# Three edits to the order of work in the attention stage: VectorE's late work in slots 0, 5 and 9, the loads of the value weights, and one matmul of the last two units

## The chip, the cores and the metric

The kernel runs on one core of a Trainium2 chip. The metric is device time in microseconds (us) of one launch; a number of launches gives a median. A core has five engines that each work through their own list of instructions in order and wait for one another by semaphores: TensorE (PE, with PEld for its weight loads), VectorE (DVE), ScalarE (ACT), GpSimd (POOL) and SyncE (SP), which here only issues DMAs. Matmuls write to PSUM, eight banks of 128 x 512 fp32; DVE and ACT read it. Everything else lies in SBUF, and what does not fit goes through DRAM by DMA.

## What is computed

One transformer block in fp32: a layernorm, attention with 32 heads of width 20 over a sliding window of 256 positions, and a gated MLP on the normed input, both added to the input.

```python
def _A_ref(x, wqkv, wo):
    H = 32; Dh = D // H; W = 256
    qkv = (x @ wqkv).reshape(B, S, 3, H, Dh).transpose(2, 0, 3, 1, 4)
    q, k, v = qkv[0], qkv[1], qkv[2]
    scores = jnp.einsum("bhqd,bhkd->bhqk", q, k) * (Dh ** -0.5)
    idx = jnp.arange(S)
    mask = (idx[:, None] - idx[None, :] >= 0) & (idx[:, None] - idx[None, :] < W)
    scores = jnp.where(mask[None, None], scores, -1e9)
    p = _softmax(scores, axis=-1)
    o = jnp.einsum("bhqk,bhkd->bhqd", p, v)
    return o.transpose(0, 2, 1, 3).reshape(B, S, D) @ wo

xn = _layernorm(x, axis=-1)
return x + _A_ref(xn, wqkv, wo) + (_gelu(xn @ w_gate) * (xn @ w_up)) @ w_down
```

S is 2048, D is 640 and the MLP is 1728 wide.

## The kernel before

An fp32 product is made of three matmuls on operands that are split into a high and a low part (`dense_steps`, L104: high by high, low by high, high by low, five column blocks each, so 15 matmuls to a group). The program has three stages: layernorm with the first projections (to about 99 us of the span), attention (to about 534 us), and the rest of the MLP with the output projection. The change touches the attention stage alone.

**Units and slots.** `attention` (L836) walks through 32 units, eight groups of four heads by four chunks of 512 positions, and each unit has `NS` = 14 slots. Time in units is read from the products of probabilities with values (ps_o on PE, `av_unit`), which come once a unit in its slot 0: unit 8 begins at 199.3 us of the profile, unit 19 at 352.5, unit 20 at 366.8. In every slot the loop first runs what falls due (`tick`), then in slots 0, 5 and 9 two pairs of score blocks for the row maxima (`pull_max`, `max_pair`), in odd slots two pieces of exponentials (`exp_piece`: two matmuls to a PSUM tile ps_e, then ACT's exp into P), then `flush`, then some matmuls of a **filler** (`pull_fill`): the dense groups of the projections and of the MLP's first tiles, which do not depend on the attention. `RATE` over `NS` says how many filler matmuls a slot gets; `debt` carries the fraction. In slot 1 one more filler matmul is pulled (L874) and in slot 3 the debt is lowered by one (L879).

**The order is written out by hand.** On PE, ACT, DVE, POOL and SP the instructions run in the order in which the program issues them (`manual_schedule`, L894), so an instruction that waits holds up all that stand behind it on its engine.

**PSUM.** Four banks (`psm`) are taken in turn by the score blocks of the maxima, two to a pair, and by a small transpose ps_n in slot 7. A pair's banks are free when DVE's two reductions (L537, junk<-ps_m) have read them. Slot 0 has up to four pairs: two ahead of the ps_o products and two behind them, so the fourth pair takes the banks of the second. Two banks (`psx`) are shared by ps_e and ps_o, two (`psd`) by the dense groups.

**What follows a dense group.** For queries and keys (`save_qk`, L262): `upper` on ACT (L291, pt<-ps_d) one slot after the group, `middle` on DVE (L287, r<-ps_d,pt), `lower` on ACT (L269, pt<-r) some slots later by the table `LAG`, `lowest` on POOL (L273, pt<-r,pt), then the stores by SP. The tile r has one buffer: the next `middle` writes r when the `lowest` before it has read it. For the MLP (`gate_up_fill`, L679): `c1` on ACT, `c2` on DVE, `c3` on ACT, `c4` on DVE (L701, gs<-ps_d,gs), `c5` on DVE (L708, he<-he,gs), then a store. DVE's part of this is called **late** work: `late` (L212) puts it on the list `lates`, and `flush` (L218) issues the list at the end of the slot.

**Loads.** SP issues all DMAs of this stage but one. `load_stack` brings queries and keys (qs, ks) back from DRAM, three units ahead, keys in slot 9 and queries in slot 12. `av_unit` stores its result from ob in slot 6 (od, sd; ob is first joined by POOL, L645). The weights of the second half of the values come through `load_v` (L296), a generator that the filler advances: its first step loads two blocks of 160 KB into two buffers wvr, each further step converts one block on ACT (L315, wvh<-wvr) and POOL (L316) and loads another; the five blocks are converted in units 5 to 8, the last two of them both in unit 8.

Of the kernel before, what the change touches and what calls it, by code (L numbers as in the profile page):

```python
# [30 lines left out]
NS = 14  # L31
# [4 lines left out]
KSLOT = 9  # L36
LAG = 3, 5, 4, 4, 4, 4, 3, 3, 4, 3, 2, 1, 1, 1
NFA = 3
HD = D // 2
HR = 5  # L40
NQD = 9
# [26 lines left out]
def block_kernel(ctx, tc, x, wqk, wv, wgu, wdo, wdl, out):  # L68
    nc = tc.nc
# [21 lines left out]
    td = [{i: dram.tile([128, 2, C], F32, name=f"td{p}{i}") for i in (1, 2, 3, 4)} for p in range(NC // 2)]  # L91
    wtd = [dram.tile([128, 4, HD], F32, name=f"wtd{q}") if q not in OWN else None for q in range(NQD)]
    rd = [dram.tile([H, C], F32, name=f"rd{c}") for c in range(NC)]
# [111 lines left out]
    now = [None]  # L205

    def at(slot, fn, *a):
        acts.setdefault(slot, []).append((fn, a))

    lates = []  # L210
# [7 lines left out]
    def flush():  # L218
        while lates:
            fn, a = lates.pop(0)  # L220
            fn(*a)

    def lag():
        return 1 if now[0] is None or now[0] < NS else LAG[now[0] % NS]

# [70 lines left out]
    def load_v(h, res, rpool=None, vt=None):  # L296
        wh = wvp.tile([128, KT, 320], F32R, name="wvh", tag="wvh")
        wl = wvp.tile([128, KT, 320], F32R, name="wvl", tag="wvl")

        if rpool is not None:  # L300
            rall = rpool.tile([128, KT, 320], F32, name="wvall")
            nc.sync.dma_start(rall, wv[h])

        def get(k):
            if rpool is not None:
                return rall[:, k, :]
            raw = wvp.tile([128, 320], F32, name="wvr", tag="wvr", bufs=2)
            nc.sync.dma_start(raw, wv[h, :, k, :])
            return raw
        raws = [get(0), get(1)]  # L310
        yield
        for k in range(KT):
            if rpool is None and 0 < k < KT - 1:
                raws.append(get(k + 1))
            nc.scalar.activation(wh[:, k, :], raws[k], AF.Copy)  # L315
            nc.gpsimd.tensor_tensor(out=wl[:, k, :], in0=raws[k], in1=wh[:, k, :].bitcast(F32), op=OP.subtract)  # L316
            if rpool is not None and k + 2 < KT:
                raws.append(get(k + 2))
            yield
        res.append((wh, wl, vt or v_tiles()))  # L320

    def v_tiles():
        vt = []
        for g in range(4):
            v = vp.tile([128, VW], F32, name="v", tag="v")
            nc.gpsimd.memset(v[:, NB * 84:NB * 84 + 12], 0.0)
            nc.gpsimd.memset(v[:, 0:NB * 84].rearrange("p (b j d) -> p b j d", j=4, d=21)[:, :, :, 20:21], 1.0)
            vt.append(v)
        return vt
# [17 lines left out]
    def run(*gens):  # L347
        for gen in gens:
            for _ in gen:
                pass  # L350
# [142 lines left out]
    def load_stack(u, which=(0, 1)):  # L493
        g, c = divmod(u, NC)
        for m in range(80 * g // 128, (80 * g + 79) // 128 + 1):
            assert all((m + 5 * i, c) in done for i in which), (u, m)

        for i in which:
            dst, src, top, again = ((qs[u % NQ], qd[c], 1, 2), (ks[u % NK], kd[c], 0, 0))[i]
            for j in (0, 2):  # L500
                for p, part, n in ((j * 32, top, 2), (j * 32 + 2 * DH, again, 1), (64 - j * 32, 0, 3)):
                    nc.sync.dma_start(dst[p:p + DH * n, j:j + 2].rearrange("p j t -> p (j t)"),
                                      src[g, part:part + n].rearrange("s (d j) t -> (s d) (j t)",
                                                                      j=4)[:, j * C:(j + 2) * C])
# [213 lines left out]
    sets = [("qk", 1), ("qk", 2), ("qk", 3), ("qk", 4), ("gu", 0)]  # L718
    sets += [("gu", f) for f in range(1, NFA)] + [("gu", NF - 1)]
    pools = (wp, None), (hp, 2)  # L720
# [92 lines left out]
    NU = NG * NC  # L813
# [4 lines left out]
    def pull_max(n, slot):  # L818
        for _ in range(n):
            x = next(stream, None)  # L820
            if x is None:
                return
            max_pair(*x)
            if x[1] == 7:
                at(slot + (MXD - slot % NS if slot >= 0 else 4), max_end, x[0])

    def tick():
        todo = [y for t in sorted(t for t in acts if t <= now[0]) for y in acts.pop(t)]
        return sorted(todo, key=lambda y: y[0] is max_end)

    def pull_fill(n):
        debt[0] += n
        while debt[0] > 0:
            debt[0] -= next(fill, 1.0)

    def attention():  # L836
        now[0] = -1
        load_stack(0)
        load_stack(1)
        load_stack(2)  # L840
        for i, (p, k, half) in enumerate((p, k, half) for p in range(NC // 2) for k in range(2) for half in range(2)):
            for j, fn in enumerate(x_sums(p, k, half)):
                m = 10 * i + j
                at(NS * (XS0 + m // XSN) + m % XSN, fn)
        for i in range(12):
            now[0] = i - 13
            for fn, a in tick():
                fn(*a)
            if i == 0:
                pull_max(1, now[0])  # L850
                pull_fill(RAMP)
                pull_max(1, now[0])
                debt[0] -= RAMP
            elif i % 2 == 0 or i == 11:
                pull_max(2, now[0])
            flush()
            pull_fill(2 * RAMP)
        pull_fill(GAP)
        for u in range(NU + 1):
            for i in range(NS):  # L860
                T = now[0] = NS * u + i
                for fn, a in tick():
                    fn(*a)
                if i in (0, 5, 9):
                    pull_max(2, T)
                if i == 0 and u:
                    if u == NU:
                        pull_fill(LAST)
                    av_unit(u - 1)
                    flush()  # L870
                    pull_max(1 if u % NC == 1 else 2, T)
                if i % 2 and i < 12 and u < NU:
                    if i == 1 and u:
                        pull_fill(1)  # L874
                        if u % NC == 1:
                            pull_max(1, T)
                    exp_piece(u, i - 1)
                    exp_piece(u, i)
                if i == 3 and u and u < NU:  # L879
                    debt[0] -= 1  # L880
                flush()
                if u + 3 < NU and i in (KSLOT, 12):
                    load_stack(u + 3, (int(i == KSLOT),))
                pull_fill(RATE / NS)
        while acts:
            now[0] += 1
            for fn, a in tick():
                fn(*a)
            flush()
        now[0] = None  # L890
        run(fill)
        assert not acts
# [147 lines left out]
    def slots(kind, q):  # L1040
        if kind == "t" and q in borrow:
            return [(quads["b", borrow[q] + i], slice(1, 2), slice(i, i + 1)) for i in range(4)]
        if (kind, q) not in quads:
            tag = place.get((kind, q))
            quads[kind, q] = (xp if tag else rp3).tile([128, 2, 4, HD], F32R, name=f"w{kind}{q}",
                                                       tag=tag or f"w{kind}{q}")
        return [(quads[kind, q], slice(0, 4), slice(0, 4))]

    def four(t):
        return t.rearrange("p k (h n) -> p (k h) n", h=2)  # L1050

    def fetch(kind, q, where="stg", eng=nc.sync):
# [9 lines left out]
        pool, bufs = (rp3, 3) if where == "stg" else (cp, 3)  # L1062
        t = pool.tile([128, 4, HD], F32, name="stg", tag=where, bufs=bufs)
        eng.dma_start(t, four(wdo[q]) if kind == "b" else wtd[q])
# [35 lines left out]
    class Job:  # L1100
# [3 lines left out]
        def load(self):  # L1104
# [5 lines left out]
            elif kind == "t":  # L1110
                t = self.t = cp.tile([128, 4, HD], F32, name="ats", tag="at", bufs=3)
                nc.sync.dma_start(t, four(wdo[i]))
# [117 lines left out]
    def terms(ns, ps):  # L1230
        work = {}
        for n in ns:
# [6 lines left out]
            if k == "e":  # L1239
                for bank, tok, h in ((2, 1, 0), (3, 1, 1), (4, 0, 0), (8, 0, 1)):  # L1240
                    mul(bank, [(t[:, tok], w13[:, z, h * HD:h * HD + HD]) for z in range(2)])
                continue
# [20 lines left out]
        for bank, lo, hi in runs:  # L1263
            for j in range(lo, hi):
                nc.tensor.matmul(ps[bank][:, 0:HD], *work[bank][j], start=bank not in begun,  # L1265
                                 stop=final[p, bank] == n and j == len(work[bank]) - 1, skip_group_check=True)
# [77 lines left out]
    order.__enter__()  # L1344
    raws_w = load_gu(NFA)
    banks = [psg.tile([128, C], F32, name="ps_g", tag=f"g{i}") for i in range(4)]
# [32 lines left out]

    raws_next = {NFA + 1: load_gu(NFA + 1)}  # L1380
    for j, f in enumerate(range(NFA, NF - 1)):
        end = f + 1 == NF - 1
# [93 lines left out]
    for n, (p, k) in enumerate(steps):  # L1476
        i = n % (NQD + 1)
# [71 lines left out]
```

## Time and profile before

| | us |
|---|---|
| median of 3 runs | 1036.77 |
| lowest and highest of them | 1036.35, 1037.86 |
| the profiled execution, its own time | 1037.18 |
| its span in the trace | 1035.5 |
| busy in the span: PE, DVE, ACT, POOL | 1028.5, 741.7, 526.9, 385.4 |

The profiled execution took 1.7 us more than its span, since a launch also has a little time ahead of the first and behind the last instruction. PE is the engine that is busy nearly always, with TensorE's clock at its full rate from end to end (PEclk 9 in all 40 slices). A matmul that waits for a semaphore is mostly not shown as idle time: the trace gives a group of neighbouring matmuls of one kind a start and a length, and a wait inside it makes the group longer than other groups of the same kind. So waits of PE are read from the length of such groups and from what DVE, ACT or a DMA finished at that time. A row of the timeline gives the start in us, the length in us, the engine, the line, the operation, output<-inputs, the shape, how many instructions it merges, and in square brackets the engine's idle time just ahead of it and what ended it.

### The profile page before, as it was taken

The numbers are of one execution on the slowest core, as the hardware profiler recorded it, in microseconds if no ns is written. First come the engines' busy times: TensorE is split into PE (matmuls) and PEld (weight loads), VectorE is DVE, ScalarE is ACT, GpSimd is POOL, SyncE is SP. The second block draws the span as 40 slices with busy tenths as digits, with TensorE's granted clock in tenths as the row PEclk, the third lists the DMA queues.
The fourth block names the chain that finished last, engine by engine and source line by source line (L and its number), as shares of the span: only waits on it lengthen the run. The fifth ranks groups of instructions, "written<-read, shape, count | busy, mean of one in ns | idle before, by whom it ended". The sixth has DMA issues, their size and how long they took to land.

```text
span 1035.5 us, 25580 instructions
## 1 busy us (share of the span) xinstructions
PE 1028.5 (99%) x9396; PEld 834.9 (81%) x9396; DVE 741.7 (72%) x2018; ACT 526.9 (51%) x1120; POOL 385.4 (37%) x623
## 2 busy tenths in 40 slices
PE   8999999999999999999999999999999999999998
PEld 8987666666787666666678888888888999999998
DVE  8755666766656677777646788776556888888887
ACT  4444767766676666676675222333234554333332
POOL 5122778888755877676551111101110000000000
PEclk9999999999999999999999999999999999999999
DMA  6542446565533354343225576762217864443333
GB/s 237 165 151 71 129 141 189 169 189 151 172 101 98 112 159 148 115 145 118 76 82 197 190 236 231 247 250 97 79 60 266 257 229 140 141 127 118 120 121 107
DMA packets 102150, 158.74 MB, mean 153 GB/s; under 512 B 14172, under 2 KB 55260, under 8 KB 102024
## 3 DMA queue, kind: packets, MB, share of 16 engines
q1 hardware_dynamic: 99640, 150.94, 45.5%
q10 hardware_dynamic: 2384, 6.16, 1.9%
q8 instruction: 74, 1.21, 0.5%
q14 instruction: 52, 0.43, 0.1%
HBM read 101.78 MB, written 54.92 MB: 151 GB/s over the span
## 4 chain that ended last, share of the span: by engine, by line
PE 97%; DVE 1%; DMA 1%; ACT 1%; issue 0%; SPq 0%; DVEq 0%; ACTq 0%
PE ps_g L993 24%; PE ps L1265 23%; PE ps_d L108 20%; PE ps_e L592 8%; PE ps_v L108 7%; PE ps_o L635 7%; PE ps_m L527 5%; PE ps_g L108 1%; PE ps_t L190 1%; DMA qs<-qd 1%; PE ps_d L370 1%; DMA xi<-x 0%; DVE junk L537 0%; DVE xi L169 0%; PE ps_n L554 0%
## 5 line engine op out<-in xcount | busy, mean ns | idle before, releaser
L537 DVE CUSTOM_DVE_ANT_0 junk<-ps_m,mask 128x320 bf16<-128x320 f32 (+2 forms) x512 | 242.6, 474 | 131.5 <-PE ps_m L527 73.6
L594 ACT ACTIVATE P<-ps_e 128x512 f32<-128x512 f32 (+2 forms) x384 | 198.5, 572 | 61.8 <-PE ps_e L592 60.0
L1265 PE MATMUL ps<-wb,at 128*128 128x320 f32 x999 | 155.9, 309 | 0.0
L1265 PEld LDWEIGHTS ps<-wb,at 128*128 128x128 f32 x999 | 148.9, 188 | 0.2
L607 POOL TENSOR_SCALAR_AFFINE_SELECT P<-P 128x256 f32<-128x256 f32 (+1 forms) x192 | 95.2, 498 | 71.2 <-ACT P L594 70.1
L592 PE MATMUL ps_e<-qs,ks 124*128 124x128 bf16 (+2 forms) x704 | 113.0, 277 | 0.1
L108 PE MATMUL ps_d<-xh,wqh 128*128 128x512 f32 x310 | 98.1, 419 | 0.0
L108 PE MATMUL ps_d<-xl,wqh 128*128 128x512 f32 x310 | 96.4, 416 | 0.0
L108 PE MATMUL ps_d<-xh,wql 128*128 128x512 f32 x310 | 96.1, 415 | 0.0
L101 POOL TENSOR_TENSOR wql<-wr,wqh 128x640 fp32r<-128x640 f32 x12 | 19.3, 1609 | 195.4 <-PE ps_g L993 171.0
L1265 PE MATMUL ps<-wt,at 128*128 128x320 f32 x552 | 88.9, 309 | 0.0
L592 PEld LDWEIGHTS <-ks 124*128 124x128 bf16 x704 | 49.8, 98 | 43.9 <-issue 28.1
L1265 PEld LDWEIGHTS ps<-wt,at 128*128 128x128 f32 x552 | 82.9, 188 | 0.1
L610 POOL TENSOR_SCALAR_AFFINE_SELECT P<-P 128x512 f32<-128x512 f32 (+1 forms) x144 | 77.3, 546 | 14.0 <-ACT P L594 14.0
L1219 ACT ACTIVATE at<-ss 128x512 fp32r<-128x512 f32 x59 | 37.3, 632 | 82.8 <-DVE ss L1098 82.7
L635 PE MATMUL ps_o<-P,v 64*32 64x320 f32 (+4 forms) x2816 | 74.2, 347 | 0.0
L273 POOL TENSOR_TENSOR pt<-r,pt 128x512 bf16<-128x512 f32 x40 | 46.8, 1169 | 59.1 <-ACT pt L269 59.1
L635 PEld LDWEIGHTS ps_o<-P,v 64*32 64x32 f32 x2816 | 50.8, 106 | 21.5 <-issue 0.9
L108 PEld LDWEIGHTS ps_d<-xh,wql 128*128 128x128 f32 x310 | 56.0, 189 | 10.7 <-issue 1.3
L1022 ACT ACTIVATE hr<-hr 128x512 f32<-128x512 f32 x20 | 12.6, 632 | 101.6 <-DVE hr L996 101.6
L108 PEld LDWEIGHTS ps_d<-xl,wqh 128*128 128x128 f32 x310 | 56.0, 189 | 10.3 <-issue 1.3
L108 PEld LDWEIGHTS ps_d<-xh,wqh 128*128 128x128 f32 x310 | 55.9, 189 | 10.4 <-issue 1.6
(197 smaller groups left out, 1984.6 us busy)
## 6 DMA issues: line engine op xcount, KB each, us to landing
hd<-he SPq DMA_DIRECT2D x50, 256.0 KB
hr<-hd SPq DMA_DIRECT2D x48, 256.0 KB
wr<-wgu SPq DMA_DIRECT2D x27, 320.0 KB
qs<-qd SPq DMA_DIRECT2D x64, 120.0 KB
ks<-kd SPq DMA_DIRECT2D x64, 120.0 KB
xi<-x SPq DMA_DIRECT2D x16, 320.0 KB
qs<-qd SPq DMA_DIRECT2D x64, 80.0 KB
ks<-kd SPq DMA_DIRECT2D x64, 80.0 KB
```

The lines of the kernel that those rows point to most:

```text
L108: nc.tensor.matmul(ps, a(k), b(k), start=n == 0, stop=n == 3 * nk - 1)
L273: nc.gpsimd.tensor_tensor(out=pt[:, l, :], in0=r, in1=pt[:, 1, :], op=OP.subtract)
L527: nc.tensor.matmul(ps[64 * h:64 * h + 64, col:col + w], q[rows, j, q0:q0 + 64], ks_, start=True, stop=True, tile_position=(64 * r, 64 * h))
L537: nc.vector.tensor_tensor_reduce(out=junk[:, 0:n], in0=ps[:, 320 - n:320], in1=mask[:, 320 - n:320], scale=1.0, scalar=NEG, op0=OP.add, op ...
L592: nc.tensor.matmul(ps[:, col:col + n], k[0:QROWS, j, kc:kc + 128], q[0:QROWS, j, q0:q0 + n], start=True, stop=True)
L594: nc.scalar.activation(pt[:, j, lo:hi], ps[:, lo:hi], AF.Exp, scale=SCALE)
L607: nc.gpsimd.affine_select(out=a, in_=a, pattern=[[0, n], [1, 128]], compare_op=OP.is_ge, fill=0.0, base=0, channel_multiplier=-1)
L610: nc.gpsimd.affine_select(out=a, in_=a, pattern=[[0, n], [-1, 128]], compare_op=OP.is_ge, fill=0.0, base=-1, channel_multiplier=1)
L635: nc.tensor.matmul(os[r][32 * j:32 * j + 32, qa:qb], v[rows, w0_:w0_ + 32], pt[rows, j, col + qa - q0:col + qb - q0], start=r not in begun ...
L993: nc.tensor.matmul(ps, i, j, start=first and n == 0, stop=n == len(work) - 1, skip_group_check=True)
L1219: nc.scalar.activation(hi[:, 3:7], s, AF.Copy)
L1265: nc.tensor.matmul(ps[bank][:, 0:HD], *work[bank][j], start=bank not in begun, stop=final[p, bank] == n and j == len(work[bank]) - 1, skip ...
```

## The change

The change has three parts.

1. In slots 0, 5 and 9 the two pairs of maxima are pulled one at a time, and between them a new function `free_bank` issues those late items that read a dense group's PSUM bank (`middle` and `c4`), with the clock set back by one slot, so that what they defer falls due one slot earlier; a second `tick` runs what is due at once. The flush at the end of slot 4 is left out (`HOLD`), so the late work of slot 4 goes behind the first pair of slot 5 where it is `middle` or `c4`, and to the flush at the end of slot 5 where it is something else.
2. `load_v` no longer issues the loads of the value weights where the filler stands, but in slot 6 of the unit, or of the next unit when the filler has passed slot 8. Slots 6 to 8 load at once.
3. In the last two units (30 and 31) the debt is lowered in slot 11 in place of slot 3.

```diff
+PAIRS = 0, 5, 9
+HOLD = (5,)
...
+    def free_bank(T):
+        now[0] = T - 1
+        ready = [y for y in lates if y[0].__name__ in ("middle", "c4")]
+        lates[:] = [y for y in lates if y not in ready]
+        for fn, a in ready:
+            fn(*a)
+        now[0] = T
...
             raw = wvp.tile([128, 320], F32, name="wvr", tag="wvr", bufs=2)
-            nc.sync.dma_start(raw, wv[h, :, k, :])
+            i = 6 if now[0] is None or now[0] < NS else now[0] % NS
+            n = 6 - i if i < 6 else NS + 6 - i if i > 8 else 0
+            if n:
+                at(now[0] + n, lambda: nc.sync.dma_start(raw, wv[h, :, k, :]))
+            else:
+                nc.sync.dma_start(raw, wv[h, :, k, :])
             return raw
...
-                if i in (0, 5, 9):
-                    pull_max(2, T)
+                if i in PAIRS:
+                    pull_max(1, T)
+                    free_bank(T)
+                    pull_max(1, T)
+                    for fn, a in tick():
+                        fn(*a)
...
-                if i == 3 and u and u < NU:
+                if u and u < NU and i == (3 if u < NU - 2 else 11):
                     debt[0] -= 1
-                flush()
+                if (i + 1) % NS not in HOLD or T + 1 >= NS * NU:
+                    flush()
```

No instruction is added or taken away. Where the order of an engine's list changes, it looks like this at three places. Line numbers of the changed kernel are higher by 10 to 15 for the same statement.

**SP in unit 8, slots 2 to 7.** The rows are DMA issues: wvr is a block of value weights, kd and qd are stores of keys and queries, td a store of sums of the input, od and sd the attention result of the unit before. Before:

```order
L502 DMA qs_177<-qd_86 60x1024
L308 DMA wvr<-wv 128x320
L282 DMA kd_91<-pt 64x3x512 x2
L775 DMA td_102<-tx 128x256
L649 DMA od_95<-ob 20x512 x4
L650 DMA sd_99<-ob 4x512
L282 DMA qd_84<-pt 16x3x512
```

Now:

```order
L517 DMA qs_177<-qd_86 60x1024
L292 DMA kd_91<-pt 64x3x512 x2
L790 DMA td_102<-tx 128x256
L664 DMA od_95<-ob 20x512 x4
L665 DMA sd_99<-ob 4x512
L321 DMA wvr<-wv 128x320
L292 DMA qd_84<-pt 16x3x512
```

The last block of value weights moves behind the four od stores and the sd store. ACT's list around the conversion of this block has the same order before and now: two exps of 128x256, wvh<-wvr, pt<-ps_d, four exps.

**DVE in unit 19, slot 0.** ISA junk,mx<-ps_m,mask is one of the two reductions of a pair (ISA mx reads its result out), and r<-ps_d,pt is `middle`; the reductions of 128x128 are the first pair, those of 128x256 the second. Before:

```order
L537 ISA mx 128x1
L537 ISA junk,mx<-ps_m,mask 128x128
L537 ISA mx 128x1
L537 ISA junk,mx<-ps_m,mask 128x256
L537 ISA mx 128x1
L537 ISA junk,mx<-ps_m,mask 128x256
L537 ISA mx 128x1
L287 TENSOR_TENSOR r<-ps_d,pt 128x512
L537 ISA junk,mx<-ps_m,mask 128x320
```

Now:

```order
L552 ISA mx 128x1
L552 ISA junk,mx<-ps_m,mask 128x128
L552 ISA mx 128x1
L297 TENSOR_TENSOR r<-ps_d,pt 128x512
L552 ISA junk,mx<-ps_m,mask 128x256
L552 ISA mx 128x1
L552 ISA junk,mx<-ps_m,mask 128x256
L552 ISA mx 128x1
L552 ISA junk,mx<-ps_m,mask 128x320
```

`middle` moves from behind the second pair to between the first and the second. The same happens in slot 0 of unit 20. In both units ACT's `lower` (pt<-r) moves too, from behind the first exps of slot 1 to ahead of the two copies of ps_o.

**DVE in unit 3, slots 4 and 5.** nm is the negated maximum. Before:

```order
L546 TENSOR_SCALAR nm_183<-mx 128x16
L547 SCALAR_TENSOR_TENSOR nm_183<-mx,nm_183 128x16
L287 TENSOR_TENSOR r<-ps_d,pt 128x512
L537 ISA junk,mx<-ps_m,mask 128x320
L537 ISA mx 128x1
```

Now:

```order
L561 TENSOR_SCALAR nm_183<-mx 128x16
L562 SCALAR_TENSOR_TENSOR nm_183<-mx,nm_183 128x16
L552 ISA junk,mx<-ps_m,mask 128x320
L552 ISA mx 128x1
L552 ISA junk,mx<-ps_m,mask 128x320
L552 ISA mx 128x1
L297 TENSOR_TENSOR r<-ps_d,pt 128x512
```

Here `middle` of slot 4 goes behind the first pair of slot 5. In units 28 and 29 it is `c5` (he<-he,gs) of slot 4 that goes behind both pairs of slot 5. On DVE the list changes at 14 places in all: seven times `middle` and twice `c4` come one pair earlier, in slots 0, 5 and 9, and the other five places are late work of slot 4.

## The prediction

> **What bounds the kernel now.** I read the page's busy times first, then busy time by stage, then who PE waited for.
>
> ```profile
> PE 1028.5 (99%) x9396; PEld 834.9 (81%) x9396; DVE 741.7 (72%) x2018; ACT 526.9 (51%) x1120; POOL 385.4 (37%) x623
> 99.00:534.00 435.00, 434.24 (x5852) 299.37 (x5859) 287.96 (x1068) 294.40 (x645) 321.85 (x546) 1.00 0.45 134
> PE ps_m L527 <- DMA qs<-qd: 0.5, 1, 0.5
> ```
>
> The second row is the attention stage (its columns: stretch, length, then busy time of PE, PEld, DVE, ACT, POOL, the clock, DMA share, GB/s). PE is busy for 434.2 of 435.0 us at full clock, and the change neither adds nor removes a matmul. So it can gain only what is hidden as waiting inside PE's groups, and it loses whatever new wait reaches PE in full: nothing behind the stage gives time back, since PE is the bound there too. The question is therefore which waits vanish and which appear. How a wait looks is shown by unit 2, where `middle` (r<-ps_d) happens to stand ahead of slot 0's reductions:
>
> ```profile
> 113.13 0.69 DVE L287 TENSOR_TENSOR r<-ps_d,pt 128x512 f32<-128x512 f32 x1 [1.31 <-ACT pt L291]
> ...
> 115.66 0.49 DVE L537 CUSTOM_DVE_ANT_0 junk<-ps_m,mask 128x320 bf16<-128x320 f32 x1
> 115.73 0.80 PE L527 MATMUL ps_m<-ks,qs 60*64 60x320 bf16 x8
> 354.86 0.47 PE L527 MATMUL ps_m<-ks,qs 60*64 60x320 bf16 x8
> ```
>
> The eight ps_m matmuls at 115.73 are pairs three and four of slot 0; the last row is the same group of unit 19. The reduction at 115.66 is the last of pair two and ends at 116.15; PE's group ends at 116.53, 0.38 behind it, and is 0.80 long. Undisturbed it takes 0.47, as in unit 19. So pair four waits until DVE is through with pair two, and what delays pair two's reductions in slot 0 beyond that point is paid by PE one for one. The same holds for the second pair of slot 9 against the second pair of slot 5.
>
> **Part 1, slot 0 of units 19 and 20: a loss.** `middle` now stands between pair one and pair two. It writes r, which must first have been read by POOL's `lowest`:
>
> ```profile
> 353.95 0.42 DVE L537 CUSTOM_DVE_ANT_0 junk<-ps_m,mask 128x256 bf16<-128x256 f32 x1
> 352.61 1.72 POOL L674 TENSOR_TENSOR wql<-wr,wqh 128x128 fp32r<-128x128 f32 x4
> 354.29 1.16 POOL L273 TENSOR_TENSOR pt<-r,pt 128x512 bf16<-128x512 f32 x1
> 355.48 0.69 DVE L287 TENSOR_TENSOR r<-ps_d,pt 128x512 f32<-128x512 f32 x1 [1.10 <-POOL pt L273]
> 356.09 0.48 DVE L537 CUSTOM_DVE_ANT_0 junk<-ps_m,mask 128x320 bf16<-128x320 f32 x1
> 367.57 1.17 POOL L273 TENSOR_TENSOR pt<-r,pt 128x512 bf16<-128x512 f32 x1
> 368.71 0.49 DVE L537 CUSTOM_DVE_ANT_0 junk<-ps_m,mask 128x320 bf16<-128x320 f32 x1
> 369.13 0.69 DVE L287 TENSOR_TENSOR r<-ps_d,pt 128x512 f32<-128x512 f32 x1
> 369.18 0.47 PE L527 MATMUL ps_m<-ks,qs 60*64 60x320 bf16 x8
> ```
>
> In unit 19 `lowest` ends at 355.45 and `middle` starts at 355.48, after 1.10 us of idle DVE. Before, pair two was done ahead of this wait (353.95 + 0.42 = 354.37), so the wait cost nothing. Now pair two is queued behind it: `middle` again at 355.48, the next reduction 0.61 later at 356.09, the second one 0.58 later (they have 256 columns) to 357.09. PE's group would end 0.38 behind that, at 357.47, against 354.86 + 0.47 = 355.33: **+2.1 us**. In unit 20 `lowest` ends at 368.74, `middle` starts there, pair two's reductions at 369.36 and 370.00, ending at 370.49; PE's group ends at 370.87 against 369.65: **+1.2 us**. By the program's order POOL has `lowest` behind the clearing of P that follows the exps of the unit before, so I do not expect it earlier; if it came, the cost would fall to the 0.6 of `middle` itself or to nothing, and each has 0 as its lower bound and 0.5 above my value as the upper, if ACT's `lower`, which now waits for `middle` ahead of the copies of ps_o, also holds up the next ps_e.
>
> **Part 1, the other places.** Seven items move by one pair in slots 5 and 9. In six of them the second pair's reductions end 0.6 later and still ahead of the next use of their banks. The seventh is c4 in unit 24. The rows are from five places of the timeline, DVE's ahead of PE's where a place has both:
>
> ```profile
> 431.80 0.49 DVE L537 CUSTOM_DVE_ANT_0 junk<-ps_m,mask 128x320 bf16<-128x320 f32 x1
> 432.60 0.47 PE L527 MATMUL ps_m<-ks,qs 60*64 60x320 bf16 x8
> 135.10 0.69 DVE L287 TENSOR_TENSOR r<-ps_d,pt 128x512 f32<-128x512 f32 x1 [0.84 <-ACT pt L291]
> 137.77 0.74 PE L527 MATMUL ps_m<-ks,qs 60*64 60x320 bf16 x8
> 485.73 1.04 DVE L708 SCALAR_TENSOR_TENSOR he<-he,gs 128x512 f32<-128x512 f32 x1
> 488.75 0.74 PE L527 MATMUL ps_m<-ks,qs 60*64 60x320 bf16 x8
> 362.22 0.67 PE L527 MATMUL ps_m<-ks,qs 60*64 60x320 bf16 x8
> 376.13 0.88 PE L527 MATMUL ps_m<-ks,qs 60*64 60x320 bf16 x8
> ```
>
> There the last reduction would end at 432.89, PE's group at 433.27 in place of 433.07: **+0.2** (0 to 0.3). The held slot 4 gains: in unit 3 DVE idles 0.84 ahead of `middle` at 135.10 with slot 5's scores ready meanwhile, in unit 28 he<-he,gs takes 1.04 ahead of them, and PE's slot 9 group pays 0.74 - 0.47 = 0.27 each time. Both go: **-0.5**. The groups at 362.22 and 376.13 (units 19 and 20, slot 9) carry 0.20 and 0.41 of waiting for a late DVE; once PE itself is 2.1 and 1.2 later, DVE has caught up: **-0.6**.
>
> **Part 2, the value weights: the largest loss.** SP is in order, and the last block now stands behind od and sd in unit 8. The rows are SP's issues, then ACT, then PE, then two pieces of the chain of waits (start, length, what) and an earlier issue of SP:
>
> ```profile
> 202.67 1.46 SPq L308 DMA_DIRECT2D wvr<-wv  x1
> ...
> 207.40 1.61 SPq L649 DMA_DIRECT2D od<-ob  x4
> 209.05 0.54 SPq L650 DMA_DIRECT2D sd<-ob  x1
> 208.31 0.47 ACT L315 ACTIVATE wvh<-wvr 128x320 fp32r<-128x320 f32 x1 [0.17 <-issue]
> 208.69 0.58 ACT L291 ACTIVATE pt<-ps_d 128x512 bf16<-128x512 f32 x1
> 209.51 1.09 ACT L594 ACTIVATE P<-ps_e 128x512 f32<-128x512 f32 x2 [0.24 <-PE ps_e L592]
> 210.40 0.62 PE L592 MATMUL ps_e<-qs,ks 124*128 124x128 bf16 x4
> 0.81 2.86 DMA xi<-x
> ...
> 143.73 5.53 DMA qs<-qd
> 145.92 1.20 SPq L308 DMA_DIRECT2D wvr<-wv  x2
> ```
>
> The load goes out at 209.05 + 0.54 = 209.6 in place of 202.67, and ACT wants the block at 208.31. From issue to landing the chain of waits has 2.86 for a block of 320 KB at the start of the kernel, and 5.53 for a part of qs in a crowded queue. A block of 160 KB behind five small stores is nearest to the first; I take 3.0, so the data is there at 212.6 and ACT stands for 4.3 us. Behind wvh on ACT are pt<-ps_d (0.38 later) and the exps of slot 9 (0.5 each, the first 0.5 behind pt): the first starts at 213.5 and ends at 214.1, the second at 214.6. They free the two banks that PE's next ps_e group takes at 210.40, so its first half waits to 214.1 and its second, which stands about half of the 0.62 behind the first, to 214.6. PE loses **3.9 us** (3.8 with 2.86, 6.4 with 5.53; 1.0 if the load took no time at all). The other four blocks land well ahead of their use. [...]
>
> What the move may bring: the qs part above was issued at 143.73, with two value blocks issued behind it at 145.92, and PE waited 0.50 for it (third row of the first fence). This wait, with a little on both sides of it, would go if the value blocks caused it. The profiled execution is also 0.41 above the median of the runs, as if most runs did not have it. I take **-0.4** (0 to -0.8). [...]
>
> **Part 3, the last two units.** One matmul more stands ahead of the exps of slots 3 to 11:
>
> ```profile
> 513.72 0.78 PE L592 MATMUL ps_e<-qs,ks 124*128 124x256 bf16 x4
> 515.33 0.60 PE L592 MATMUL ps_e<-qs,ks 124*128 124x256 bf16 x4
> 526.18 0.79 PE L592 MATMUL ps_e<-qs,ks 124*128 124x256 bf16 x4
> ```
>
> Slot 5's group takes 0.78 and 0.79 where an unhindered one takes 0.60: PE waits there for ACT's exps. With a filler matmul more ahead of it, that waiting is filled: **-0.35** (0 to -0.4).
>
> **Sum:** 3.9 + 2.1 + 1.2 + 0.2 - 0.5 - 0.6 - 0.4 - 0.35 = +5.5. Made against the profiled execution's own 1037.18 this gives 1042.7 us; the median of the runs shown, 1036.77, is 0.4 lower, which is the term for qs.
>
> **The rivals.** (a) *The value load costs nothing*: SP reaches slot 6 sooner, with nothing of the load at 202.67 in its way, and ACT has its block in time. For it: the issue at 202.67 took 1.46 of SP's time. Against it: SP stood idle ahead of od at 207.40, so what it waits for there, POOL's join of ob, is late by itself. Time: 1042.7 - 3.9 = 1038.8. (b) *Slot 0 costs nothing*: POOL's `lowest` is done before pair one is, as it would be with less in POOL's queue. Against it: in unit 19 POOL runs four wql parts of the next head's weights from 352.61 to 354.33, right up to `lowest`, and the change leaves them there. Time: 1042.7 - 3.3, and the 0.6 of slot 9 then stays, so 1040.0. (c) *Only the gains arrive*, the other side: (a) and (b) have one root, POOL running some 4 us earlier in the stage, since od waits for POOL's join and `middle` for POOL's `lowest`; it decides once POOL ends `lowest` before 353.4 and the join before 203. Then 1037.18 + 0.2 - 0.5 - 0.4 - 0.35 = 1036.1, faster than before but by less than 0.2%; with slot 9 and the whole 0.8 as well 1035. (d) *A slower load*: the block meets the stores of queries behind it and takes nearer 5.5: 1045.2.
>
> **How the numbers follow.** My forecast 0.63 (1042.7, within 1041 to 1044); (a) 0.11; (b) 0.11; (c) 0.05; (d) 0.10. The range 1038.8 to 1045.2 leaves out (c) and the tails. Less than 0.2%, 2.1 us, is about what a measurement of this kernel cannot tell from no change. Slower by more than that is the forecast, (b), (d) and half of (a): 0.89. Half of (a) and most of (c) are the same: 0.09. Faster: 0.02.
>
> **What would show it.** In the changed profile ACT's last wvh<-wvr waits some 4 us for a DMA, and the next ps_e group of PE is 4 us long; r<-ps_d in slot 0 of units 19 and 20 sits between the pairs with POOL ahead of it, and PE's ps_m group behind ps_o is 2.6 and 1.7 long. The ps_m groups of slot 9 in units 3, 19, 20 and 28 are back at 0.47, that of unit 24 is at 0.7. The forecast is wrong if the wvh wait is under 1 us, or if the ps_m groups in slot 0 stay at 0.47.

## The result and the profile after

| | before | after |
|---|---|---|
| median of six runs each, us | 1036.72 | 1044.20 |
| lowest to highest, us | 1036.35 to 1037.86 | 1042.41 to 1044.86 |
| the profiled execution, us | 1037.18 | 1043.58 |
| its span, us | 1035.5 | 1041.9 |

The changed kernel is slower: the ratio of its runs to those of before is 1.0067, with a 95% interval of 1.0054 to 1.0080, which is 6.9 us (5.6 to 8.3); the two medians are 7.5 apart. Between the profiled executions it is 6.4 us, and 6.3 of them lie in the attention stage (441.30 against 435.00). Three views of the changed kernel show it. The busy times of the page (engine, busy time, share of the span, instructions):

```profile
PE 1029.9 (99%) x9396; PEld 836.1 (80%) x9396; DVE 739.6 (71%) x2018; ACT 527.1 (51%) x1120; POOL 383.8 (37%) x623
```

The stretch of the attention stage, in the columns of the prediction:

```profile
99.10:540.40 441.30, 435.60 (x5858) 300.42 (x5864) 285.85 (x1069) 294.43 (x644) 320.21 (x546) 1.00 0.45 132
```

PE's waits in that stretch (who waited for whom, us in total, times, longest):

```profile
PE ps_e L607 <- ACT P L609: 2.9, 1, 2.9
PE ps_m L542 <- DVE mx L552: 2.4, 4, 1.4
```

PE runs as many matmuls as before. In the stage it stands 5.7 us idle (441.30 - 435.60) where it stood 0.8, and its busy time is 1.4 us longer for the same work. Nearly all of the idle time has two owners: one stop of 2.9 for ScalarE's exps and four that sum to 2.4 for VectorE's reductions. The longer busy time has a third cause, below.

PE's matmuls stand in the same order in both kernels but for the lone one of the last two units, so each can be matched with itself, and the distance between its two start times tells where the time goes. It changes at these places:

| place | distance ahead (us) | behind | step | predicted |
|---|---|---|---|---|
| unit 3, slot 9 | +0.08 | -0.19 | -0.27 | -0.27 |
| unit 4, slot 5 (the wait for qs) | -0.17 | -0.97 | -0.80 | -0.4 |
| unit 8, ps_e behind wvh | -0.94 | +3.65 | +4.59 | +3.9 |
| unit 19, slot 0 | +3.59 | +5.75 | +2.16 | +2.1 |
| unit 20, slot 0 | +5.73 | +6.97 | +1.24 | +1.2 |
| unit 19, slot 9 | +5.73 | +5.74 | 0 | -0.2 |
| unit 20, slot 9 | +6.97 | +6.56 | -0.41 | -0.4 |
| unit 24, slot 9 | +6.54 | +6.55 | 0 | +0.2 |
| unit 28, slot 9 | +6.51 | +6.25 | -0.26 | -0.27 |
| units 30 and 31 and the last ps_o | +6.25 | +6.45 | +0.20 | -0.35 |

Between these places it drifts by less than 0.1. At the end it is 6.4, the difference of the two spans.

**Unit 8.** The load's piece in the chain of waits (start, length, what):

```profile
208.67 2.37 DMA wvr<-wv
```

SP, ACT and PE from the timeline:

```profile
208.09 0.54 SPq L665 DMA_DIRECT2D sd<-ob  x1
208.67 0.44 SPq L321 DMA_DIRECT2D wvr<-wv  x1
211.06 0.47 ACT L330 ACTIVATE wvh<-wvr 128x320 fp32r<-128x320 f32 x1 [3.87 <-DMA wvr<-wv]
211.44 0.58 ACT L301 ACTIVATE pt<-ps_d 128x512 bf16<-128x512 f32 x1
211.92 1.07 ACT L609 ACTIVATE P<-ps_e 128x512 f32<-128x512 f32 x2
212.56 1.07 PE L607 MATMUL ps_e<-qs,ks 124*128 124x128 bf16 x4 [2.95 <-ACT P L609]
213.17 2.16 PE L110 MATMUL ps_d<-xh,wql 128*128 128x512 f32 x4
```

The load goes out behind sd, at 208.67, and lands 2.37 later; ACT has stood 3.87 for it, and PE 2.95 behind ACT. But the step here is 4.59. The rest is in the last rows: four ps_d matmuls take 2.16, where the same four take 1.21 in a kernel that is shown below. The busy time by stretch names the reason in its third column from the right, the granted clock:

```profile
209.50:212.50 3.00, 0.11 (x1) 0.04 (x1) 0.38 (x1) 1.44 (x4) 0.86 (x1) 0.97 0.75 212
212.50:213.50 1.00, 0.94 (x5) 0.67 (x5) 0.86 (x4) 0.81 (x3) 0.38 (x2) 0.50 0.70 211
213.50:214.50 1.00, 1.00 (x4) 0.81 (x3) 0.36 (x2) 1.00 (x3) 0.92 (x4) 0.50 0.60 178
214.50:215.50 1.00, 1.00 (x3) 0.78 (x3) 0.00 (x0) 0.28 (x1) 1.00 (x4) 0.50 0.73 254
215.50:216.50 1.00, 1.00 (x19) 0.56 (x17) 0.00 (x0) 0.00 (x0) 1.00 (x1) 0.89 0.73 171
```

Right behind the stop PE works at half clock, and nowhere else in the stage. In slices of 0.2 us the half clock runs from 212.32 to 215.73: 3.41 us. That shows in the mean clock of the execution too, 0.998: 3.41 x 0.5 is 0.16% of 1041.9.

**Slot 0 of units 19 and 20.** DVE, POOL and PE from the timeline, unit 19 and then unit 20:

```profile
357.90 1.15 POOL L283 TENSOR_TENSOR pt<-r,pt 128x512 bf16<-128x512 f32 x1
359.08 0.69 DVE L297 TENSOR_TENSOR r<-ps_d,pt 128x512 f32<-128x512 f32 x1 [2.27 <-POOL pt L283]
360.16 0.29 PE L542 MATMUL ps_m<-ks,qs 60*64 60x320 bf16 x1 [1.39 <-DVE mx L552]
360.74 0.33 PE L542 MATMUL ps_m<-ks,qs 60*64 60x320 bf16 x3 [0.28 <-DVE mx L552]
...
373.29 1.17 POOL L283 TENSOR_TENSOR pt<-r,pt 128x512 bf16<-128x512 f32 x1
374.49 0.69 DVE L297 TENSOR_TENSOR r<-ps_d,pt 128x512 f32<-128x512 f32 x1 [0.84 <-POOL pt L283]
375.64 0.29 PE L542 MATMUL ps_m<-ks,qs 60*64 60x320 bf16 x1 [0.41 <-DVE mx L552]
376.28 0.33 PE L542 MATMUL ps_m<-ks,qs 60*64 60x320 bf16 x3 [0.35 <-DVE mx L552]
```

`middle` stands between the pairs and waits for POOL's `lowest`, which ends right ahead of it (359.05 and 374.46). PE's pair four waits twice, once for each reduction of pair two. These four waits are the 2.4 of the table of waits.

**Slot 9.** The groups of units 3, 24 and 28 in the changed kernel, all at 0.47 (before: 0.74, 0.47 and 0.74):

```profile
137.84 0.47 PE L542 MATMUL ps_m<-ks,qs 60*64 60x320 bf16 x8
439.13 0.47 PE L542 MATMUL ps_m<-ks,qs 60*64 60x320 bf16 x8
495.26 0.47 PE L542 MATMUL ps_m<-ks,qs 60*64 60x320 bf16 x8
```

### The profile page after: what moved, and what is told of

The parts are those of the page before. It is cut to its first block, busy times and chain, and to the rows that moved or that the text cites. A ratio compares the mean times of both kernels' runs of the same rounds, so it can differ in the third digit from the quotient of the medians.

```text
span 1041.9 us, 25573 instructions
## 1 busy us (share of the span) xinstructions
PE 1029.9 (99%) x9396; PEld 836.1 (80%) x9396; DVE 739.6 (71%) x2018; ACT 527.1 (51%) x1120; POOL 383.8 (37%) x623
## 3 DMA queue, kind: packets, MB, share of 16 engines
q8 instruction: 74, 1.21, 0.5%
## 4 chain that ended last, share of the span: by engine, by line
PE 95%; DVE 1%; ACT 1%; DMA 1%; POOL 1%; SPq 0%; issue 0%; ACTq 0%; DVEq 0%
PE ps_g L1013 23%; PE ps L1285 23%; PE ps_d L110 20%; PE ps_e L607 8%; PE ps_v L110 7%; PE ps_o L650 6%; PE ps_m L542 5%; PE ps_g L110 1%; PE ps_t L192 1%; ACT P L609 1%; PE ps_d L385 1%; SPq L517 0%; DMA xi<-x 0%; DVE xl L201 0%; DMA wvr<-wv 0%
## 5 line engine op out<-in xcount | busy, mean ns | idle before, releaser
L542 PE MATMUL ps_m<-ks,qs 60*64 60x320 bf16 (+3 forms) x1472 | 61.9, 260 | 2.6 <-DVE mx L552 2.4
```

The costliest lines, as they stand in the source:

```text
L542: nc.tensor.matmul(ps[64 * h:64 * h + 64, col:col + w], q[rows, j, q0:q0 + 64], ks_, start=True, stop=True, tile_position=(64 * r, 64 * h))
```

## The experiments

Each kernel below was timed against the kernel before on the same chip, and profiled once. "Step" is again the change of the distance between matched matmuls, against the profiled execution of before.

**Each part alone.** First the order of VectorE, with the loads and the debt as before:

```diff
-            i = 6 if now[0] is None or now[0] < NS else now[0] % NS
...
-                at(now[0] + n, lambda: nc.sync.dma_start(raw, wv[h, :, k, :]))
+            nc.sync.dma_start(raw, wv[h, :, k, :])
...
-                if u and u < NU and i == (3 if u < NU - 2 else 11):
+                if i == 3 and u and u < NU:
```

> Only the order of VectorE is changed (middle and c4 between the pairs in slots 0, 5 and 9, slot 4 held); loads and debt as before. Theory (the steps of the changed kernel's trace): +2.2 in slot 0 of unit 19, +1.2 in slot 0 of unit 20, -0.3 in slot 9 of unit 3, -0.3 in slot 9 of unit 28, -0.4 in slot 9 of unit 20: +2.4, 1039.1 us against 1036.7, granted clock 1.000, and the wait for qs ahead of unit 4 stays in the profile. Rival: that wait goes with the order too, +1.6, 1038.3.

Measured: 1040.51 us, ratio 1.0031 (1.0019 to 1.0043). The steps of units 3, 20 (both) and 28 are as in the whole change. Unit 19 steps by 3.74 instead of 2.16. PE's rows there:

```profile
356.53 0.29 PE L537 MATMUL ps_m<-ks,qs 60*64 60x320 bf16 x1 [1.38 <-DVE mx L547]
357.10 0.33 PE L537 MATMUL ps_m<-ks,qs 60*64 60x320 bf16 x3 [0.28 <-DVE mx L547]
```

And the stretches from there on:

```profile
356.50:358.50 2.00, 1.69 (x12) 0.97 (x11) 1.43 (x6) 1.27 (x3) 1.63 (x2) 1.00 0.62 184
358.50:359.50 1.00, 1.00 (x5) 0.89 (x3) 0.53 (x3) 0.90 (x2) 0.92 (x3) 0.50 0.45 112
359.50:360.50 1.00, 1.00 (x4) 0.40 (x3) 0.97 (x3) 0.18 (x1) 1.00 (x2) 0.50 0.22 63
360.50:361.50 1.00, 1.00 (x6) 0.83 (x6) 0.47 (x2) 0.38 (x1) 0.27 (x1) 0.50 0.92 284
```

The waits are the same as in the whole change (1.38 and 0.28), and 1.4 us after PE has taken up work again the clock halves, again for 3.41 us. So the expected waits were there, and 1.6 on top of them; five of the six runs show the clock of 0.998. Why the same waits halved the clock here and not in the profile of the whole change, where they are 1.39 and 0.28, no run shows. The wait for qs in unit 4 is gone here, although the loads stand where they stood before: against the theory. Two steps that the whole change does not have, +0.2 in unit 6 and +0.7 in unit 10, come from short waits of PE for qs (0.2) and for VectorE's nm (0.4).

The loads alone (the three other changes of `attention` undone):

> Only the value weights' loads are held to slot 6; the order and the debt are as before. Theory (the sum of the steps seen in the changed kernel's trace): ScalarE waits some 3.9 us for the last block in unit 8, PE idles 3.0 to 3.1 us for ps_e, then runs some 3.4 us at a granted clock of 0.50, which costs another 1.5; together +4.6, less 0.8 for the wait for qs that goes: +3.8, so 1040.5 us against 1036.7. Rival 1: the half clock is not tied to this wait, so it is absent here: +2.3, 1039.0. Rival 2: the wait for qs went for another reason (the order, or chance) and stays here: +4.6, 1041.3.

Measured: 1042.45 us, ratio 1.0052 (1.0038 to 1.0066). The runs fall in two groups: 1039.98 and 1040.43 at a clock of 1.000, and 1042.45, 1042.56 and 1043.54 at 0.998 or 0.997. The profiled execution is one of the first, and shows what the stop costs by itself (PE's rows, and the stretches behind the stop at full clock):

```profile
212.75 0.87 PE L607 MATMUL ps_e<-qs,ks 124*128 124x128 bf16 x4 [2.85 <-ACT P L609]
213.31 1.21 PE L110 MATMUL ps_d<-xh,wql 128*128 128x512 f32 x4
```

```profile
212.70:213.70 1.00, 0.84 (x6) 0.57 (x6) 0.30 (x1) 1.00 (x3) 0.38 (x2) 1.00 0.65 193
213.70:214.70 1.00, 1.00 (x6) 0.84 (x5) 0.00 (x0) 1.00 (x3) 1.00 (x4) 1.00 0.69 174
```

Its step in unit 8 is 3.23 with a stop of 2.85; the changed kernel's was 4.59 with one of 2.95. Rival 1 was half right: the half clock does not come every time. Where a profile below has it, it stands behind this stop; for the three runs here only the mean clock is known, so that it stood there too is inferred. The theory's 0.8 of gain was wrong, and its 1040.5 is too low by more than that.

The debt alone:

> Only the lone matmul of the last two units is repaid in slot 11. Theory (the changed kernel's trace): the 0.17 of waiting ahead of ps_e in slot 7 of each unit goes, and as much or more comes back behind slot 11 (0.26 in unit 30) and in the last ps_o group (0.2): +0.1, so 1036.8 against 1036.7, no change that can be told. Rival, as predicted: only the gains arrive, -0.35, 1036.35.

Measured: 1037.25 us, ratio 1.0001 (0.9992 to 1.0009). In unit 30 the ps_e groups of this kernel, and below them those of before, show where it goes:

```profile
513.51 0.61 PE L602 MATMUL ps_e<-qs,ks 124*128 124x256 bf16 x4
518.01 0.87 PE L602 MATMUL ps_e<-qs,ks 124*128 124x128 bf16 x4
```

```profile
513.72 0.78 PE L592 MATMUL ps_e<-qs,ks 124*128 124x256 bf16 x4
518.30 0.61 PE L592 MATMUL ps_e<-qs,ks 124*128 124x128 bf16 x4
```

The first group is 0.17 shorter and the second 0.26 longer. The wait has moved to the slot in which the matmul is repaid. The wait for qs is gone in this kernel too, and here nothing ahead of unit 30 differs from before.

**What the held loads bring.** As the loads alone, but the last block goes where it went before:

```diff
-            if n:
+            if n and k < KT - 1:
```

> The value weights' loads held to slot 6 but for the last block, which is loaded where it was; order and debt as before. Theory: the two first blocks, moved behind the qs parts of unit 3, take the 0.8 away and the last block costs nothing: 1035.9 us against 1036.7, no idle PE in unit 8, granted clock 1.000. Rival: the wait for qs is chance and not caused by the value blocks: the same time as before, 1036.7, and the wait is there in some executions.

Measured: 1037.40 us, ratio 1.0006 (0.9997 to 1.0015). The rival holds: holding the blocks brings nothing that these runs can tell (the interval is -0.3 to +1.6 us). PE does not stop in unit 8, and the clock is 1.000.

**How the half clock depends on the stop.** As the loads alone, but the last block is issued from within the store of unit 8: ahead of sd (the edit shown), ahead of the fourth od, or ahead of the third.

```diff
+                go = lambda: nc.sync.dma_start(raw, wv[h, :, k, :])
+                if k == KT - 1:
+                    last.append(go)
...
+            if last:
+                last.pop()()
             nc.sync.dma_start(sd[c][4 * g:4 * g + 4, :], ob[DH::32, :])
```

Ahead of sd:

> As the kernel with only the loads held, but the last block is issued between the four od stores and sd, some 0.55 us sooner. Theory A, the half clock follows from any PE idle of over about 2 us: PE idles 2.5, half clock again for some 3.4 us: +2.5 + 1.5 - 0.8 = +3.2, 1039.9 us. Theory B, the half clock needs an idle time nearer to 3 us or more: clock 1.000 throughout and +2.5 - 0.8 = +1.7, 1038.4 us.

Ahead of the fourth od:

> As the kernel with only the loads held, but the last block is issued between the third and the fourth od store. PE stops for some 1.9 us. [...]

Ahead of the third od:

> As the kernel with only the loads held, but the last block is issued between the second and the third od store, some 1.5 us sooner. Theory: ScalarE waits 2.3 to 2.4 us, PE idles some 1.5 us, the clock stays at 1.000 and the loss is the idle time alone: +1.5 - 0.8 = +0.7, 1037.4 us. Rival: the half clock comes after every stop of PE behind this wait: +1.5 + 1.5 - 0.8 = +2.2, 1038.9 us.

PE's first row behind the stop, in three fences in that order:

```profile
212.15 0.86 PE L613 MATMUL ps_e<-qs,ks 124*128 124x128 bf16 x4 [2.19 <-ACT P L615]
```

```profile
211.78 0.86 PE L613 MATMUL ps_e<-qs,ks 124*128 124x128 bf16 x4 [1.83 <-ACT P L615]
```

```profile
211.30 0.86 PE L613 MATMUL ps_e<-qs,ks 124*128 124x128 bf16 x4 [1.49 <-ACT P L615]
```

| last block | PE's stop (us) | half clock in the profile | step in unit 8 | runs at 0.998 or less | median (us) | ratio |
|---|---|---|---|---|---|---|
| ahead of the third od | 1.49 | none | 1.88 | 0 of 7 | 1039.43 | 1.0026 (1.0015 to 1.0037) |
| ahead of the fourth od | 1.83 | 212.54 to 215.95 | 3.77 | 3 of 5 | 1040.47 | 1.0033 (1.0020 to 1.0046) |
| ahead of sd | 2.19 | 213.46 to 216.87 | 4.10 | 5 of 5 | 1041.97 | 1.0048 (1.0035 to 1.0061) |
| behind sd (loads alone) | 2.85 | none | 3.23 | 3 of 5 | 1042.45 | 1.0052 (1.0038 to 1.0066) |
| behind sd (whole change) | 2.95 | 212.32 to 215.73 | 4.59 | 4 of 6 | 1044.20 | 1.0067 (1.0054 to 1.0080) |

The clocks of single runs are means over the whole run, and the stops are those of the profile; in the whole change a half clock in another run can also have followed the waits of unit 19, as it does with the order alone. Without the half clock the step is the stop and 0.4. With it, it is 1.3 to 1.6 more. The half clock lasts 3.41 us each time and starts during the stop or up to 1.3 us behind its end. By the mean clocks (0.997 or 0.998 against 1.000) it came in all five runs with the stop of 2.19, and in some runs and not in others with the stops of 1.83, 2.85 and 2.95. So it is not the stop's length alone that decides: theory A's "any PE idle of over about 2 us" and theory B's "nearer to 3 us" both fall. A stop of 1.83 had the half clock behind it in its profile, and one of 2.85 had not. What decides it beyond the length, no run shows. With the block ahead of the third od the stop is the theory's 1.5 and the clock is 1.000 (0.999 in two of the seven runs); the median is 0.9 above that of before plus the step, within the interval. The 0.8 that the expectations of the loads alone, of sd and of the third od subtract is the wait for qs, and falls with it.

**Slot 0.** As the order alone, but in slot 0 the late work stays behind both pairs:

```diff
-                    free_bank(T)
+                    if i:
+                        free_bank(T)
```

> As the kernel with only the order changed, but in slot 0 the late work stays behind both pairs. Theory: the losses of units 19 and 20 go, and with them the 0.4 won back in unit 20; what stays is -0.3 in unit 3 and -0.3 in unit 28: 1036.1 us against 1036.7. Rival: the loss is not from middle's wait for GpSimd but from the later slots, and +1 or more stays.

Measured: 1036.43 us, ratio 0.9995 (0.9986 to 1.0004). PE has no step in slot 0 and no wait in the stage that reaches the list of waits; the steps of units 3 and 28 are -0.27 and -0.26, and the only other one is that the wait for qs is gone here too. The two losses are slot 0's.

To tell the wait for POOL from the move itself, the next kernel keeps the order of the first, but lets r alternate with a buffer that is first used in unit 21:

```diff
-        r = qkp.tile([128, C], F32, name="r", tag="r", bufs=1)
+        nr[0] += 1
+        if now[0] is not None and now[0] >= NS and nr[0] % 2:
+            r = hp.tile([128, C], F32, name="he", tag="he", bufs=2)
+        else:
+            r = qkp.tile([128, C], F32, name="r", tag="r", bufs=1)
```

> As the kernel with only the order changed, but r alternates between its own buffer and one that stands unused until unit 21 (the one of he), so that middle in slot 0 need not wait for GpSimd's reading of the r before it. Theory: the loss of slot 0 is that wait; without it middle costs its own 0.6 at most, which is hidden in unit 19 (+0.0) and shows by 0.5 in unit 20; with the two gains of 0.3 and no half clock the time is that of before: 1036.7 us, within 0.3. Rival: the loss comes from putting middle ahead of pair two as such (its place on VectorE and ScalarE, not the wait for GpSimd): +2 or more stays, 1039 or more.

Measured: 1037.24 us, ratio 1.0002 (0.9993 to 1.0011). DVE's `middle` and the next reduction in unit 19, and PE's group behind them in units 19 and 20:

```profile
354.03 0.69 DVE L303 TENSOR_TENSOR he<-ps_d,pt 128x512 f32<-128x512 f32 x1
354.64 0.41 DVE L553 CUSTOM_DVE_ANT_0 junk<-ps_m,mask 128x256 bf16<-128x256 f32 x1
355.75 0.47 PE L543 MATMUL ps_m<-ks,qs 60*64 60x320 bf16 x8
370.08 0.78 PE L543 MATMUL ps_m<-ks,qs 60*64 60x320 bf16 x8
```

`middle` starts without a wait, at the place in the order where it lost 2.2 before, and PE's group is undisturbed in unit 19 and 0.31 longer in unit 20. Of the 3.4 of slot 0 the wait for POOL's reading of r is 3.1; `middle` itself is 0.3. (This profile also has a step of 1.1 in unit 9, where ScalarE waited 1.0 for a store of kd, which no other profile shows, and two of 0.3, in slot 0 of units 2 and 12, where VectorE stands still for 0.5 between two reductions; why it does is not shown.)

**The whole change without its two losses** (slot 0 as above, the last block as before):

> The whole change, but without its two losses: the late work stays behind both pairs in slot 0, and the last value block is loaded where it was. Theory: nothing else in the change costs anything, 0.3 is won in units 3 and 28 each, and the moved blocks and the debt bring nothing: 1036.2 us against 1036.7. Rival: the parts add up to something more than each alone (the held blocks with the held slot): 1037.5 or more.

Measured: 1037.47 us, ratio 1.0001 (0.9992 to 1.0009): no loss is left, and the gain of 0.5 that the profile shows in units 3 and 28 is less than these runs can tell. PE's waits in its attention stage are this one row:

```profile
PE ps_m L542 <- DMA qs<-qd: 0.4, 1, 0.4
```

That is the wait for qs, here with four of the blocks held; it stood in the profile of before with the blocks as they were, and it is gone with the debt alone, where they are as they were too.

No version here beats the kernel before by more than its runs can tell. The nearest is the order without slot 0.

## Why the prediction came out as it did

The sign and the two places were right, and the size came out near (+5.5 forecast, +6.4 between the profiled executions, +6.9 by the runs), partly by luck, because errors cancelled: the load was priced 0.6 too high, and the half clock behind its stop was missing.

- **Slot 0** (+2.1 and +1.2): 2.16 and 1.24, by the mechanism that was given. Two experiments confirm it, one by taking the move away and one by taking the wait away. Rival (b) is out.
- **The value load** (+3.9): the mechanism was right, and its term was mis-sized twice. The block landed in 2.37, not 3.0, so PE stopped for 2.95 and the step by itself would be some 3.3. And the half clock behind the stop, 1.3 in this profile, was not in the sum at all. Rivals (a), (c) and (d) are out: it does cost, and the load was faster.
- **The wait for qs** (-0.4): no gain. It vanished from the profiles of four kernels that leave the loads alone (the order alone, the debt alone, the order without slot 0, the two buffers for r) and of five that hold all of them (the whole change, the loads alone and its three variants), and was there in one that holds four of them (the repaired one); the other that holds four (the last block early) shows most of it gone. So the place of the loads does not decide it. The prediction took the middle of its range, 0 to -0.8, and the end at 0 gave the right number. What does bring the wait stays open. The -0.80 of the table above belongs to the profiled execution of before, which had this wait; the ratios of the runs show no such gain (1.0001 with the debt alone, 1.0006 with the last block early).
- **Slot 9 of units 3 and 28** (-0.5): -0.53. **Of units 19 and 20** (-0.6): -0.41. Unit 20 as said; in unit 19 the ps_m group is short, but the ps_e behind it comes no sooner (+5.73 ahead, +5.74 behind). **Of unit 24** (+0.2): nothing; the group is at 0.47, though c4 does stand between the pairs.
- **The debt** (-0.35): +0.2 and no difference in its runs. The term counted the waits that go and not the slot in which the matmul comes back, where ps_e waits in turn.

Against the medians the sum is then 3.3 + 2.2 + 1.2 - 0.5 - 0.4 + 0.2 = 6.0 without the half clock, and 1.3 to 1.6 more with it; four of the six runs show a clock of 0.998. The measured interval, 5.6 to 8.3, holds both.

## What to carry to other kernels

Before a loaded buffer is moved to a later slot, look for the consumer that does not move with it: five blocks were held, four landed well ahead of their use (the trace shows no wait of ACT ahead of converting them), and the fifth was wanted by ACT at 207.19 (211.06 - 3.87), 1.5 us before it was issued. An operation that is moved ahead of others in an in-order queue brings its waits with it, and here these cost more than its duration (3.1 against 0.3). And the price of PE's four stops of 1.83 to 2.95 us in unit 8 was here the stop, about 0.4 and, where a stretch at half clock came with it, 1.3 to 1.6 us more; 15 of the 21 runs of these four kernels show a mean clock of 0.998 or less.

## What the runs showed of the hardware

The half clock was not expected. In the attention stage of four profiles it came with a stop of PE: one stop of 1.83, of 2.19 and of 2.95, and two of 1.38 and 0.28 close together. It lasted 3.41 us each time at a granted clock of 0.50, and began between 0.24 us ahead of the end of the stop (2.95) and 1.4 us behind it (1.38 and 0.28). In other profiles it did not come: not with a stop of 1.49, not with one of 2.85, and not with the two of 1.39 and 0.28 in unit 19 of the whole change.

The mean clocks of the runs agree with that. With the stop of 1.49 it is 0.999 or 1.000 in all seven runs; with the stops of 1.83 and 2.85 it is 0.997 or 0.998 in three of five and 1.000 in the other two. So the same kernel has the half clock in one run and not in the next, and neither the length of a stop nor the sum of two close together sorts the cases. What does sort them, no run shows.

There is a second spread, of another origin. In three profiles (the debt alone, the last block early, the repaired one) PE waits 0.6 to 1.2 in the last matmul stage, for VectorE, which stands behind ScalarE and a DMA of wtd. These executions took 1038.4 to 1038.7, where the lowest of the same kernels took 1036.3 to 1036.6. From the first of them, PE's wait and then ScalarE's:

```profile
PE ps L1275 <- DVE xr L1298: 1.2, 1, 1.2
ACT wt L1089 <- DMA stg<-wtd: 3.2, 1, 3.2
```

No part of the change touches that stage. The runs of the kernel before spread as widely (1036.37 to 1038.72 in one series), though its one profile does not show this wait. So a gain of half a us cannot be told by a median of these runs.
